# One core, a layer norm with a state-space convolution and eight experts: the convolution as three chains that take VectorE in turn, its bank handed out by readiness, its first steps in block two

## The chip, the cores and the metric

One core of one Trainium2 chip runs the whole program in one launch. The metric is the device time of one execution in microseconds (us). The kernel before took 2315.51, 2316.52 and 2318.74 us in three runs; the median is 2316.52 us.

## The reference

What is computed, cut to what matters (2048 tokens, width 512, 128 states, 8 experts of hidden width 1792, and K = 8, so that every token goes to every expert):

```
u: x = A_u                                # 2048 x 512
xn = layernorm(x)
# S4: a kernel of 2048 taps per channel, convolved causally with xn
dt = exp(log_dt); logdA = dt*(A_re + 1j*A_im); dB = dt*(B_re + 1j*B_im)
K[d, l] = sum_n (C[d,n] * exp(logdA[d,n]*l) * dB[d,n]).real
s4 = irfft(rfft(xn, 4096) * rfft(K, 4096))[:2048] + xn*Dskip
# experts
gates = softmax(xn @ w_gate)
moe = sum_e gates[:, e] * (silu(xn @ w1[e]) @ w2[e])
out = x + s4 + moe
```

## The kernel before, in words

**Products.** Every matmul operand is split into a high and a low half-precision part, and three products of the parts stand for one in single precision. The tokens are cut into 4 blocks `tb` of 512, the hidden width of an expert `e` into 7 pieces `pr` of 256, which are taken in 4 steps `d` (two pieces in a step, one in the last). `block(e, tb, d)` (L1969) forms the first layer's step with seven products instead of eight, from sums and differences of quarters of w1 and of the tokens; it writes three banks `hb0` to `hb2`, and ACT and VectorE make the halves `ahl` from them: ACT copies (L1996, L2011), the Silu into `fa`, `scB`, `scC` (L1504), the high half (L1508), and VectorE the low half (L1517). The second layer, `y` (L1471 to L1473, through `pop`), follows some slots later and reads `ahl`. In six "strong" blocks, (6,1), (6,2) and all four of expert 7, the second layer is made with seven products too: `block2` (L1827), `pop2` (L1726, output `z`), `evacuate2` (L1774). Their operands (`hs`, `f`, `ev`, `w2x`) lie in a second pool, p2, which `open_second` (L591) opens in the place of the pool p4 once S4 is done.

**The order is written by hand.** The program runs under a manual schedule: each engine's instructions stand in the order in which the Python code issues them. A block's step is four slots; `slot` (L1642) issues the matmuls of a product, some units of `y`, the high halves that are due, the low ones, pieces of weights that are being split (`work_on`, L641) and then S4 in the background: `bg_run` (L1396) takes the next steps of a generator as long as the estimated VectorE time of the slot, a fixed share of its estimated TensorE time, is not used up. A step yields its estimated VectorE cost, or `None` where it has to wait for another slot.

**Weights.** w1 comes raw in 512 KB pieces. Before, `piece_w1` (L538) formed the four sums of quarters in a tile `tw` (one 512-wide and two 256-wide VectorE operations, L504 to L506), split the three raw quarters (L493 on ACT, L496 on VectorE), and then split the sums. The pieces of experts 6's and 7's strong first blocks use `piece_w1x` (L568): the raw quarters are split first, the four sums are then made in their place (four 256-wide operations, L581), and split.

**S4** goes through 32 chunks `c` of 16 channels. VectorE makes a table of powers (`s4_tables`, L826: `ta`, `tt`, `table`), TensorE generates the taps from it (`kgen`, L871), ACT reads them, they go through DRAM (`s4_kernel_turn`, L892) and come back as `kt`; a power of two scales them (`s4_kscale` on VectorE, L902, from a total that TensorE sums up, `tot_k`, L183), ACT and VectorE split them (`kh`, L911 and L916). TensorE transforms them (`kf`, L954) and the tokens (`uf`, L940); VectorE multiplies in the short direction (`s4_conv`, L962 to L1007: `v3`, `k4`, `s3`, `z`), ACT and VectorE split `z` (`zh`, L1013, L1018), TensorE transforms back (`yp`, L1028), ACT copies it out (`ysb`, L1036), and SP's queue stores it (`ys`, L1037). All of `kgen`, `tot_k`, `kf`, `uf`, `yp`, the gates (`lg`) and the transposes share one small PSUM bank, tag "s4" of `ps_s`. Before, one generator `s4_pe` (L1094) asked for it in a fixed order, kf(c), yp(c-1), kgen(c+2), tot_k(c+2), uf(c+1), and `together` (L1057) ran VectorE's part of one c (table c+2, convolution c, tokens c+1) to its end before the next c. The first steps (basis, twiddles, dt, the DFT matrix) were part of the background too, `s4_all` (L1209).

At the end, `s4_final` (L1684) needs all `ys`; `gneg` (L2075) is the first VectorE operation on negated gates for the second half's evacuations.

## Time and profile before

| | |
|---|---|
| runs | 2315.51, 2316.52 (median), 2318.74 us |
| the profiled execution | 2316.77 us, span 2315.0 us (1.77 us lie outside of it) |
| mean granted TensorE clock | 0.998 |
| TensorE matmuls (PE) | busy 2297.5 us, 99% |
| weight loads (PEld) | 1644.3 us, 71% |
| VectorE (DVE) | 1885.4 us, 81% |
| ScalarE (ACT) | 1520.4 us, 66% |
| GpSimd (POOL) | 340.1 us, 15% |

How to read it: busy is the time in which an engine has an instruction in it. Matmuls are pipelined, so that the busy time of one is longer than the distance to the next; the distance of their starts is read from a timeline. A window's line gives the span, each engine's busy time in it with the number of instructions, the granted clock (1.00 is 2.4 GHz, 0.50 is 1.2 GHz), the DMA engines' share and the rate. A wait names the engine and line that waited, and what released it.

### The profile page before, as it was taken

Reading aid. Unit: us, or ns where it says so; the run is one execution under the profiler, and the core shown is the slowest. Engines: PE = TensorE matmul, PEld = TensorE weight load, DVE = VectorE, ACT = ScalarE, POOL = GpSimd, SP = SyncE. Lnnn points to the kernel's source line nnn. Section 1 sums busy time; section 2 is a strip of 40 time slices with the busy share of each in tenths; the row PEclk is TensorE's granted clock in tenths of the full one; section 3 lists DMA queues with packets and bytes.
Section 4 is the critical chain, followed back from the end, with each engine's and each line's share of the span. In section 5 each row is a group of like instructions: output and inputs, shape, how many; then the busy total and the mean of one; then the engine's idle time right before and its main releaser. Section 6 shows DMA issues by size and latency. Waiting matters only on the chain.

```text
span 2315.0 us, 51747 instructions
## 1 busy us (share of the span) xinstructions
PE 2297.5 (99%) x20809; PEld 1644.3 (71%) x20809; DVE 1885.4 (81%) x3984; ACT 1520.4 (66%) x2718; POOL 340.1 (15%) x397
## 2 busy tenths in 40 slices
PE   8999999999999999999999999999999999999999
PEld 4666666666666666666666666666666689779998
DVE  8864889989999899997999989998867664775445
ACT  7676666566665666666666666766667566775655
POOL 0001001121111211011110111111111111132111
PEclk9999999999999999999999999999999999999999
DMA  8597355774666746556465654576665563586353
GB/s 278 178 262 197 102 147 122 158 155 85 156 145 139 152 89 151 141 123 139 81 148 149 136 116 100 138 180 145 137 159 135 131 148 69 118 205 120 88 109 66
DMA packets 326817, 323.82 MB, mean 140 GB/s; under 512 B 183760, under 2 KB 221008, under 8 KB 326096
## 3 DMA queue, kind: packets, MB, share of 16 engines
q1 hardware_dynamic: 270272, 226.32, 33.3%
q0 software_dynamic: 56016, 93.94, 25.7%
q8 instruction: 162, 2.65, 0.5%
q14 instruction: 79, 0.65, 0.1%
q10 hardware_dynamic: 288, 0.26, 0.0%
HBM read 209.22 MB, written 66.58 MB: 119 GB/s over the span
## 4 chain that ended last, share of the span: by engine, by line
PE 95%; DVE 2%; ACT 2%; issue 1%; DMA 1%; POOL 0%; SPq 0%; DVEq 0%; ACTq 0%; POOLq 0%
PE hb L1488 34%; PE y L1471 13%; PE y L1473 13%; PE y L1472 13%; PE hb L1843 8%; PE z L1761 7%; PE hb L2047 2%; PE kgen L871 1%; PE yp L1028 1%; PE kf L954 1%; PE uf L940 1%; DMA scC<-sE 0%; PE tp L284 0%; DMA ut0c<-in_u_dram 0%; DVE hs L1876 0%
## 5 line engine op out<-in xcount | busy, mean ns | idle before, releaser
L1488 PE MATMUL hb<-xop,w1s 128*128 128x256 f16 x7350 | 865.6, 273 | 1.4 <-ACT scC L1996 1.0
L1488 PEld LDWEIGHTS <-w1s 128*128 128x128 f16 x7350 | 707.9, 98 | 133.6 <-issue 3.1
L1471 PE MATMUL y<-w2s,ahl 128*128 128x512 f16 x1456 | 552.1, 379 | 0.0
L1472 PE MATMUL y<-w2s,ahl 128*128 128x512 f16 x1456 | 552.1, 379 | 0.0
L1473 PE MATMUL y<-w2s,ahl 128*128 128x512 f16 x1456 | 552.1, 379 | 0.0
L1699 POOL DMA_DIRECT2D scC<-sE x124 | 111.6, 900 | 1346.7 <-ACT sE L1996 895.8
L1473 PEld LDWEIGHTS <-ahl 128*128 128x128 f16 x1456 | 142.2, 98 | 172.0
L1472 PEld LDWEIGHTS <-ahl 128*128 128x128 f16 x1456 | 142.3, 98 | 130.6
L1471 PEld LDWEIGHTS <-ahl 128*128 128x128 f16 x1456 | 142.3, 98 | 130.5
L1843 PE MATMUL hb<-xop,w1s 128*128 128x128 f16 x3528 | 212.7, 219 | 2.6 <-ACT scC L1853 1.6
L1504 ACT ACTIVATE fa<-hb,sc 128x512 f32<-128x512 f32 (+1 forms) x204 | 129.8, 636 | 126.2 <-PE hb L1488 125.8
L1843 PEld LDWEIGHTS <-w1s 128*128 128x128 f16 x3528 | 204.9, 98 | 8.0 <-issue 3.4
L1761 PEld LDWEIGHTS <-hs 128*128 128x128 f16 x1764 | 168.7, 98 | 20.0 <-DVE hs L1876 0.8
L1517 DVE SCALAR_TENSOR_TENSOR ahl<-fa,sc,ahl 128x512 f16<-128x512 f32 (+1 forms) x214 | 146.1, 683 | 30.8 <-ACT ahl L1508 30.6
L2011 ACT COPY hb<-hb 128x512 f32<-128x512 f32 x100 | 51.7, 517 | 173.7 <-PE hb L1488 173.5
L1699 POOL DMA_DIRECT2D scB<-sE x123 | 106.2, 863 | 401.5 <-ACT scB L1996 227.3
L1508 ACT ACTIVATE ahl<-fa,sc 128x512 f16<-128x512 f32 (+1 forms) x214 | 143.7, 672 | 7.7 <-DMA xnd<-xn 0.8
L859 DVE TENSOR_TENSOR table<-ta,tt 128x64 f32<-128x64 f32 (+2 forms) x192 | 132.0, 688 | 5.8
L853 DVE TENSOR_TENSOR ta<-table,zr 128x64 f32<-128x64 f32 (+2 forms) x192 | 131.8, 686 | 5.7
L995 DVE TENSOR_TENSOR s<-s,tm 128x672 f32<-128x672 f32 (+6 forms) x224 | 127.7, 570 | 7.7
L856 DVE TENSOR_TENSOR tt<-table,zi 128x64 f32<-128x64 f32 (+2 forms) x192 | 130.4, 679 | 0.0
L994 DVE TENSOR_TENSOR tm<-v,k 128x672 f32<-128x672 f32 (+6 forms) x224 | 126.6, 565 | 4.4
(332 smaller groups left out, 3299.6 us busy)
## 6 DMA issues: line engine op xcount, KB each, us to landing
xop<-xd SPq DMA_DIRECT2D x210, 256.0 KB, 3.7
pp<-in_w_dram SPq DMA_DIRECT2D x98, 512.0 KB, 4.4
raw<-in_w_dram SPq DMA_DIRECT2D x70, 512.0 KB, 4.3
oacc<-ye POOLq DMA_DIRECT2D x110, 256.0 KB, 6.3
scC<-sE POOLq DMA_DIRECT2D x87, 256.0 KB, 3.7
scB<-sE POOLq DMA_DIRECT2D x87, 256.0 KB, 3.6
raw<-in_w_dram SPq DMA_DIRECT2D x52, 256.0 KB, 3.6
raw<-in_w_dram SPq DMA_DIRECT2D x104, 128.0 KB, 4.0
```

What stands on the lines that cost most here:

```text
L853: V.tensor_tensor(ta, tin, zrv, op=ALU.mult)
L856: V.tensor_tensor(tt, tin[:, ::-1], ziv, op=ALU.mult)
L859: V.tensor_tensor(tout, ta, tt, op=ALU.add)
L1471: T.matmul(y, lhs[0], w2s[pr][:, 0, fh, :], start=(c == 0), stop=False)
L1472: T.matmul(y, lhs[0], w2s[pr][:, 1, fh, :], start=False, stop=False)
L1473: T.matmul(y, lhs[1], w2s[pr][:, 0, fh, :], start=False, stop=(c == NF - 1))
L1488: T.matmul(dst[:, q, :], w1s[pr][:, a, ORDER[e][wo], k * P:(k + 1) * P], xop[:, xo, b, k, :], start=(first_mm and q == 0 and n == 0), stop ...
L1508: S.activation(ahl[:, 0, :n], fa, AF.Copy, scale=scales[e][:, 3:4])
L1517: V.scalar_tensor_tensor(ahl[:, 1, :n], fa, sc[:, 3:4], ahl[:, 0, :n], op0=ALU.mult, op1=ALU.subtract)
L1699: nc.gpsimd.dma_start(dst, src, accum_op=ALU.add)
L1761: T.matmul(acc, t[:, a, q, :], w2_op(pr, p, b), start=(first and k == 0), stop=(c == NPR and k == 2), skip_group_check=True)
L1843: T.matmul(dst[:, q, :], w1s[pr][:, x, ORDER[e][wo], k * P:(k + 1) * P], xop[:, xo, b, k, tk], start=(first_mm and q == 0 and m == 0), sto ...
```

## The change

S4's matmuls come from four generators, each with its own conditions, which queue for the small bank; a copy out of the bank takes place at the earliest a slot after the matmuls. VectorE's part is three streams (tokens, tables, convolution), and `in_turn` takes a step of the first one that can go, in a sequence that depends on whether the tables are four chunks ahead. The total of a chunk's rows is column 256 of the next chunk's `kgen` bank, so `tot_k` is gone. The transformed taps get a tile of their own (`kr`), the convolution works on `k3`, and its result stands in `s3`; `kt` and `kh` have two buffers, the raw inputs `s4raw` one. One slot less lies between the scale and the high half of `kh`, and one less between the halves of `zh`. The basis, the twiddles and dt are issued in slots 30 to 44, which lie in block two. All w1 pieces take the form in which the sums replace the raw quarters, `tw` is gone, and every expert uses the order of products that the strong ones had. `fa` and `ev` move from their own buffers into others: `fa` into two of p4, and once p2 is open `fa` and `ev` into the twelve that `hs` rotates through. The six strong blocks are the same.

```diff
     def bank_free():
         if bank["out"]:
-            if clock["two"]:
+            if clock["two"] or bank["set"] == clock["slot"]:
                 return False
             take_bank()
         return clock["slot"] > bank["at"]
...
-    def w1_sums(e, pr, raw):
-
-        clock["dve"] += 1.4
-        tw = sb.tile([P, 4, 2 * P], F32, tag="tw", name=f"tw{e}_{pr}", bufs=1)
-        V.tensor_tensor(tw[:, 0:2, :], raw[:, 3:4, :].to_broadcast([P, 2, 2 * P]), raw[:, 0:3:2, :], op=ALU.subtract)
-        V.tensor_tensor(tw[:, 2, :], raw[:, 2, :], tw[:, 0, :], op=ALU.subtract)
-        V.tensor_tensor(tw[:, 3, :], raw[:, 1, :], tw[:, 2, :], op=ALU.subtract)
-        return tw
+    def w1_sums(raw):
+
+        clock["dve"] += 1.5
+        for o, x, y in ((0, 3, 0), (3, 3, 2), (2, 2, 0), (1, 1, 2)):
+            V.tensor_tensor(raw[:, o, :], raw[:, x, :], raw[:, y, :], op=ALU.subtract)
...
     def s4_kernel(c):
+        take_bank(lambda: s4_kernel_out(c))
+        kg = ps_s.tile([P, 512], F32, tag="s4", name=f"kgen{c}")
+        s4["kgen"] = kg
+        if c:
+            T.matmul(kg[:, 256:257], ones, s4["krow", c - 1].bitcast(BF16)[:, 1::2], start=True, stop=True)
+        if c == NCH:
+            return
...
     def s4_raw(g):
-        raw = p4.tile([P, 6, GD], F32, tag="s4raw", name=f"s4raw{g}", bufs=2)
+        raw = p4.tile([P, 6, GD], F32, tag="s4raw", name=f"s4raw{g}", bufs=1)
...
-    def together(gens):
...
+    def in_turn(x, tables, conv):
+
+        gens = {"x": x, "tables": tables, "conv": conv}
         while gens:
...
+            behind = s4.get("tabs", 0) - s4.get("zs", 0) < 4
+            for n in ("x", "tables", "conv") if behind else ("x", "conv", "tables"):
+                cost = next(gens[n], "end") if n in gens else None
+                if cost == "end":
+                    gens.pop(n)
+                elif cost is not None:
+                    yield cost
+                    break
+            else:
                 yield None
...
+    asked = []
+
     def bank_wait():
-        while not bank_free():
+        me = object()
+        asked.append(me)
+        while not bank_free() or asked[0] is not me:
             yield None
+        asked.pop(0)
...
+    def s4_pe_kf():
+        for c in range(NCH):
+            if c:
+                yield from until(("k3", c - 1))
+            yield from until(("kl", c))
+            yield from bank_wait()
+            s4_kf(c)
+            s4["kf", c] = now()
+            yield None
...
     def s4_ksplit(c):
...
-        if c:
-            yield from until(("kl", c - 1), more=0)
+        if c > 1:
+            yield from until(("kl", c - 2), more=0)
         s4_kernel_turn(c)
-        yield from bank_wait()
-        s4["kst", c] = pow2_total(s4["krow", c], 1, f"k{c}", lambda: s4.update({("read", c): now()}))
...
         yield from until(("read", c), more=0)
         s4_kscale(c)
         yield 0.6
-        yield None
-        if c:
-            yield from until(("kf", c - 1), more=0)
+        if c > 1:
+            yield from until(("kf", c - 2), more=0)
         s4_khigh(c)
...
         s4_zhigh(c)
         yield None
-        yield None
         s4_zlow(c)
...
-        polled.append(s4_pe())
-        for c in range(-2, NCH):
...
+        polled.extend((s4_pe_kf(), s4_pe_kernel(), s4_pe_back(), s4_pe_uf()))
+        yield from in_turn(s4_x_stream(), s4_table_stream(), s4_conv_stream())
...
-            fa = sb.tile([P, 2, TH], F32, tag="fa", name=f"fa{e}_{tb}_{d}_{fh}{th}")[:, :n]
+            late = "pool" in second_half
+            fa = (second_half["pool"] if late else p4).tile([P, 2, TH], F32, tag="hs" if late else "fa",
+                                                            name=f"fa{e}_{tb}_{d}_{fh}{th}", bufs=NHS if late else 2)[:, :n]
...
+    for n in range(30, 45):
+        at(n, lambda: next(first_part, None))
```

ACT, around the last chunk of S4. `ysb31` is the copy of the last chunk's result, `ahl5_3_3_00` and `fa5_3_3_00` belong to the last step of block (5,3), `sc6` and `w2s` to expert 6. Before:

```order
L1036 ACTIVATE ysb30_23885<-yp30_23580,ksc30_22633 128x256
L1036 ACTIVATE ysb31_23901<-yp31_23888,ksc31_23227 128x256
L1933 COPY hb1_103<-hb0_102 128x512
L1504 ACTIVATE scC6_0_3_23837<-scC6_0_3_23837,sc6_20970 128x256
L1508 ACTIVATE ahl6_0_3_11_23943<-scC6_0_3_23837,sc6_20970 128x256
L1940 COPY hb2_104<-hb1_103 128x512
L1865 ACTIVATE f11_6_1_0_24021<-hb0_102,sc6_20970 128x512
```

And of the change, on the same engine at the same tile `ysb31`:

```order
L1036 ACTIVATE ysb31_23103<-yp31_23039,kscale_139 128x256
L2003 COPY hb1_103<-hb0_102 128x256
L1504 ACTIVATE scC5_3_2_22998<-scC5_3_2_22998,sc5_17653 128x512
L1508 ACTIVATE ahl5_3_2_11_23115<-scC5_3_2_22998,sc5_17653 128x512
L498 ACTIVATE w2s1_96<-raw6_1_1_23031,sc6_20982 128x1024
L2013 COPY hb2_104<-hb1_103 128x256
L1504 ACTIVATE fa5_3_3_00_23152<-hb0_102,sc5_17653 128x256
L1508 ACTIVATE ahl5_3_3_00_23154<-fa5_3_3_00_23152,sc5_17653 128x256
```

The last result of S4 moved from the first strong block, (6,1), to the last step of block (5,3), a whole block earlier, and six instructions behind it stands the first tile of the second pool, `fa5_3_3_00`. Counted over the whole order of TensorE, the last `yp` stands at matmul 13,395 and stood at 13,959; the first `z` stands at 14,253 in both.

VectorE and ACT around the scale of chunk 3. `it_k3` and `ksc3` are the scale, `kh3` the taps of chunk 3 split, `table` and `ta5` the table of chunk 5, `ye` and `ahl` belong to the experts. Before, VectorE, and the ACT rows around the reader:

```order
L189 TENSOR_SCALAR it_k3_5922<-st_k3_5780 128x1
L190 TENSOR_SCALAR ksc3_5921<-it_k3_5922 128x1
L194 TENSOR_SCALAR ksc3_5921<-ksc3_5921 128x1
L1517 SCALAR_TENSOR_TENSOR ahl1_2_0_01_5868<-fa1_2_0_01_5866,sc1_2895,ahl1_2_0_01_5868 128x512
L834 COPY table_3319<-s4w2_5093 128x2x16
...
L1446 ACTIVATE ye1_4_6041<-y1_1_0_5166,gse1_3266 128x512
L1446 ACTIVATE ye1_5_6044<-y1_1_1_5170,gse1_3266 128x512
L911 ACTIVATE kh3_6048<-kt3_5594,ksc3_5921 128x256
L1996 COPY scC1_2_1_6070<-hb2_104 128x512
```

And of the change, the same rows of VectorE and of ACT:

```order
L845 TENSOR_TENSOR table_3068<-ta5_1_5531,tt5_1_5532 128x2x32x2
L192 TENSOR_SCALAR it_k3_5583<-st_k3_5504 128x1
L193 TENSOR_SCALAR kscale_139<-it_k3_5583 128x1
L197 TENSOR_SCALAR kscale_139<-kscale_139 128x1
L887 TENSOR_TENSOR ksb4_5506<-ksb4_5506,dskq_131 128x4
...
L1508 ACTIVATE ahl1_1_2_11_5613<-scC1_1_2_5472,sc1_3058 128x512
L181 COPY st_w2_0_5580<-tot_w2_0_5581 128x1
L909 ACTIVATE kh3_5624<-kt3_5255,kscale_139 128x256
L2013 COPY hb2_104<-hb1_103 128x256
L1504 ACTIVATE fa1_1_3_00_5648<-hb0_102,sc1_3058 128x256
```

The scale now stands one slot, not two, ahead of the ACT instruction that reads it, and the copy of bank `hb2`, on which TensorE's next product waits, stands right behind that instruction.

## Rows read from the trace of the kernel before

**Rows 1.** The first part of the page: busy time, share of the span and number of instructions of each engine.

```profile
PE 2297.5 (99%) x20809; PEld 1644.3 (71%) x20809; DVE 1885.4 (81%) x3984; ACT 1520.4 (66%) x2718; POOL 340.1 (15%) x397
```

**Rows 2.** Windows from 20 us to the end (us from the span's start: width, then busy time of each engine with its instructions, granted clock, DMA share, GB/s), cut where S4 begins to weigh on VectorE, at its last result and at the strong blocks.

```profile
20.00:260.00 240.00, 240.00 (x1695) 151.04 (x1693) 168.13 (x411) 170.64 (x279) 16.95 (x21) 1.00 0.70 207
260.00:520.00 260.00, 260.00 (x2207) 174.70 (x2206) 234.09 (x528) 167.00 (x312) 39.14 (x45) 1.00 0.61 142
...
780.00:1040.00 260.00, 259.97 (x2223) 175.59 (x2221) 247.66 (x511) 165.71 (x309) 37.44 (x43) 1.00 0.56 129
...
1300.00:1560.00 260.00, 259.72 (x2165) 175.29 (x2163) 245.51 (x537) 169.04 (x317) 35.61 (x41) 1.00 0.57 131
1560.00:1780.00 220.00, 220.00 (x1828) 149.10 (x1826) 173.14 (x364) 148.26 (x279) 31.30 (x36) 1.00 0.64 148
...
1838.00:1980.00 142.00, 140.44 (x1795) 127.03 (x1795) 86.10 (x158) 89.72 (x153) 22.70 (x26) 1.00 0.47 99
1980.00:2037.00 57.00, 55.92 (x426) 40.16 (x424) 42.62 (x67) 46.73 (x72) 10.38 (x12) 1.00 0.62 168
2037.00:2315.00 278.00, 273.17 (x3570) 250.87 (x3567) 152.30 (x269) 170.06 (x292) 55.13 (x63) 1.00 0.53 109
sum 2295.00, PE 2287.09 PEld 1635.58 DVE 1871.57 ACT 1509.13 POOL 339.40; mean PE 207.92 PEld 148.69 DVE 170.14 ACT 137.19 POOL 30.85
```

**Rows 3.** TensorE's waits over the whole span: the line that waited, what released it, us in total, times, longest.

```profile
PE tp L359 <- ACT xhl L349: 7.7, 1, 7.7
PE hb L1843 <- ACT scC L1853: 1.6, 2, 1.3
...
PE hb L1488 <- ACT scC L1996: 1.0, 2, 0.7
...
PE hb L1488 <- ACT hb L2011: 0.3, 1, 0.3
```

**Rows 4.** Timeline of TensorE in block (6,0) (start us, us, line, operation, operands, shape, count): the matmuls of a product between units of `y`.

```profile
1779.06 4.09 PE L1488 MATMUL hb<-xop,w1s 128*128 128x256 f16 x36
1782.99 0.38 PE L1471 MATMUL y<-w2s,ahl 128*128 128x512 f16 x1
...
1785.58 2.78 PE L1488 MATMUL hb<-xop,w1s 128*128 128x256 f16 x24
```

**Rows 5.** Lines of VectorE with the forms apart (count, busy us, mean ns of one, idle before): the sums of w1.

```profile
L504 DVE TENSOR_TENSOR tw<-raw 128x512 f32<-128x512 f32 x42 | 28.9, 688 | 0.7
L505 DVE TENSOR_TENSOR tw<-raw,tw 128x256 f32<-128x256 f32 x42 | 17.8, 425 | 1.4
L506 DVE TENSOR_TENSOR tw<-raw,tw 128x256 f32<-128x256 f32 x42 | 17.8, 425 | 1.4
L581 DVE TENSOR_TENSOR raw<-raw 128x256 f32<-128x256 f32 x28 | 11.8, 425 | 0.9
```

**Rows 6.** The tiles `kgen` and `yp` (count, duration ns min/median/max, first and last start us).

```profile
L871 PE MATMUL kgen<-table x2048: 218/219/244, 310.8 to 1733.9; 128*32 128x64 f32 x187
L1028 PE MATMUL yp<-zh,dfth x384: 218/219/220, 411.4 to 1832.5; 128*128 128x128 f16 x192
```

**Rows 7.** Timelines of TensorE (first two rows) and of ACT (the next two) in the first strong block, with the idle time before an instruction in brackets, and one wait of VectorE over the whole span.

```profile
1863.94 1.47 PE L1761 MATMUL z<-w2x,hs 128*128 128x256 f16 x12
1866.76 2.17 PE L1843 MATMUL hb<-xop,w1s 128*128 128x128 f16 x36 [1.34 <-ACT scC L1853]
...
1864.16 2.18 ACT L493 ACTIVATE w2x<-raw,sc 128x1024 f16<-128x1024 f32 x2
1866.24 0.47 ACT L1853 COPY scC<-hb 128x384 f32<-128x384 f32 x1
...
DVE gneg L2075 <- DMA ys<-ysb: 11.7, 1, 11.7
```

**Rows 8.** Lines of ACT with the forms apart (columns as in rows 5, behind the idle time what ended it).

```profile
L1504 ACT ACTIVATE fa<-hb,sc 128x256 f32<-128x256 f32 x50 | 23.7, 474 | 11.0 <-PE hb L1488 11.0
L2011 ACT COPY hb<-hb 128x256 f32<-128x256 f32 x25 | 9.0, 359 | 12.8 <-PE hb L1488 12.8
L1036 ACT ACTIVATE ysb<-yp,ksc 128x256 f32<-128x256 f32 x32 | 15.0, 467 | 15.5 <-PE yp L1028 10.3 <-DMA ys<-ysb 5.2
L1013 ACT ACTIVATE zh<-z 128x512 f16<-128x512 f32 x32 | 20.0, 625 | 2.4 <-DVE z L1007 2.4
```

**Rows 9.** Line 1037, the stores of S4's results: the issue on SP's queue (ns min/median/max, first and last start us), and the time from issue to landing.

```profile
L1037 SPq DMA_DIRECT2D ys<-ysb x32: 586/612/964, 419.7 to 1837.4; - x32
DMA to landing us min/median/max: 3.3/4.6/11.3
```

**Rows 10.** A line of TensorE (columns as in rows 5).

```profile
L871 PE MATMUL kgen<-table 128*32 128x64 f32 x2048 | 35.2, 221 | 0.1
```

**Rows 11.** A wait of SP's queue over the whole span, for the buffers of raw weights (columns as in rows 3).

```profile
SPq L480 <- ACT pp L489: 213.9, 43, 17.0
```

**Rows 12.** Windows of the first 20 us, columns as in rows 2.

```profile
6.80:10.20 3.40, 0.00 (x0) 0.00 (x0) 2.42 (x12) 1.17 (x3) 0.00 (x0) 0.63 1.00 341
10.20:13.60 3.40, 1.21 (x11) 0.95 (x12) 3.01 (x10) 2.27 (x4) 0.00 (x0) 0.50 0.96 293
13.60:17.00 3.40, 3.28 (x32) 2.77 (x29) 2.89 (x9) 3.33 (x6) 0.00 (x0) 0.50 0.95 304
17.00:20.40 3.40, 3.06 (x28) 2.21 (x27) 2.54 (x4) 3.40 (x7) 0.00 (x0) 0.87 1.02 375
```

More of the change, by code (lines that the diff above doesn't have):

```diff
@@ L112, in take_bank @@
             bank["at"] = clock["slot"]
-        bank["out"] = out
+        bank["out"], bank["set"] = out, clock["slot"]
     def bank_free():
         if bank["out"]:
-            if clock["two"]:
+            if clock["two"] or bank["set"] == clock["slot"]:
                 return False
@@ L144, in s4_moe_kernel @@
     dt_all = p4.tile([P, D], F32, bufs=1, name="dt_all")
-    dfth = p4.tile([P, 2, 8, P], F16, bufs=1, name="dfth")
+    dfth = p4.tile([P, 2, 2, 2, P], F16, bufs=1, name="dfth")
+    dftb = cp.tile([P, 2, 2, 2, P], F16, name="dftb")
+    kscale = cp.tile([P, NCH, 2], F32, name="kscale")
     def load_rest():
@@ L634, in can @@
             return False
-        if it.sums and len(it.steps) == it.n:
-            return not live["tw"]
-        if it.sums and len(it.steps) == 1:
-            return now() > it.at + (it.made[0] > 1)
+        if it.load is not None and it.n > 1 and len(it.steps) == 1 and it.made[1] == "w1":
+            return now() > it.at + (it.made[0] > 1 and "pool" not in second_half)
         return len(it.steps) == it.n or it.load is None or now() > it.at
     def work_on(limit):
+        if limit == 2 and bank["out"] and now() > bank["set"] + 2:
+            limit = 1
         clock["two"], n2 = False, limit
@@ L658, in work_on @@
                 break
-            if it.sums and len(it.steps) == it.n:
-                live["tw"], it.at = True, now()
             low = it.steps.pop(0)(it.raw)
@@ L667, in work_on @@
             if low:
-                lows.append((low, last, it.sums and last, it.made))
+                lows.append((low, last, it.made))
             elif last and it.load is not None:
@@ L678, in work_lows @@
         while lows:
-            low, last, sums, what = lows.pop(0)
+            low, last, what = lows.pop(0)
             low()
@@ L893, in s4_kernel_turn @@
         ksb = s4["ksb"]
-        kt = p4.tile([P, 4, 4 * NI], F32, tag="kt", name=f"kt{c}", bufs=1)
+        kt = p4.tile([P, 4, 4 * NI], F32, tag="kt", name=f"kt{c}", bufs=2)
         kd = kds[c % 2]
@@ L902, in s4_kscale @@
     def s4_kscale(c):
-        ks = s4["ks", c] = p4.tile([P, 2], F32, tag="ksc", name=f"ksc{c}", bufs=4)
+        ks = s4["ks", c] = kscale[:, c, :]
         pow2_scale(ks[:, 0:1], s4["kst", c], f"k{c}")
@@ new lines, in s4_pe_kernel @@
+    def s4_pe_kernel():
+        for c in range(NCH + 1):
+            if c < NCH:
+                yield from until(("tab", c))
+            if c:
+                yield from until(("ke", c - 1))
+            yield from bank_wait()
+            s4_kernel(c)
+            s4["kn", c] = now()
+            if c < NCH:
+                polled.append(s4_ksplit(c))
+            yield None
+    def s4_pe_kf():
+        for c in range(NCH):
+            if c:
+                yield from until(("k3", c - 1))
+            yield from until(("kl", c))
+            yield from bank_wait()
+            s4_kf(c)
+            s4["kf", c] = now()
+            yield None
@@ L1131, in s4_pe, with s4_pe_uf, s4_pe_back @@
+    def s4_pe_uf():
+        for c in range(NCH):
+            if c:
+                yield from until(("v3", c - 1))
+            yield from until(("ul", c))
+            yield from bank_wait()
+            s4_uf(c)
+            s4["uf", c] = now()
+            yield None
+    def s4_pe_back():
+        for c in range(NCH):
+            yield from until(("zl", c))
+            yield from bank_wait()
+            s4_back(c)
+            s4["back", c] = now()
+            yield None
         yield from bank_wait()
@@ L1138, in s4_ksplit @@
         yield 0.3
-        yield from hold(now())
-        if c:
-            yield from until(("kl", c - 1), more=0)
+        if c > 1:
+            yield from until(("kl", c - 2), more=0)
         s4_kernel_turn(c)
-        yield from bank_wait()
-        s4["kst", c] = pow2_total(s4["krow", c], 1, f"k{c}", lambda: s4.update({("read", c): now()}))
-        s4["total", c] = now()
         yield None
-        while ("read", c) not in s4:
-            bank_free()
-            if ("read", c) not in s4:
-                yield None
         yield from until(("read", c), more=0)
@@ L1437, in s4_moe_kernel @@
     units = []
-    ORDER = [(0, 1, 2, 3, 6, 5, 4) if (e, 0) in strong else tuple(range(7)) for e in range(E)]
+    ORDER = (0, 1, 2, 3, 6, 5, 4)
     ys = {}
@@ L1776, in evacuate2 @@
         g0, g1 = gates_e[e][:, i0:i0 + 1], second_half[e, "gneg"][:, i1:i1 + 1]
-        ev = second_half["pool"].tile([P, 2, TH], F32, tag="ev", name=f"ev{e}_{tb}_{a}", bufs=1)
+        ev = second_half["pool"].tile([P, 2, TH], F32, tag="hs", name=f"ev{e}_{tb}_{a}", bufs=NHS)
         t1, t7 = ev[:, 0, :], ev[:, 1, :]
@@ L1869, in high @@
         def high(p, f):
-            h = second_half["pool"].tile([P, 2, 4, P], F16, tag="hs", name=f"hs{p}_{e}_{tb}_{d}", bufs=12)
+            h = second_half["pool"].tile([P, 2, 4, P], F16, tag="hs", name=f"hs{p}_{e}_{tb}_{d}", bufs=NHS)
             S.activation(flat(h[:, 0]), flat(f), AF.Copy, scale=scales[e][:, 3:4])
```

268 lines of the change are left out of this document (111 added, 157 removed).

## The prediction

> **What bounds the kernel now.** I read the first part of the page for the engines, then windows for the stages, then TensorE's waits, then timelines where TensorE stood. The page gives TensorE 99% and VectorE 81% [rows 1]; the windows say it by stage. From 20 us to the end TensorE is busy 2287.09 of 2295.00 us [rows 2]: 7.91 us idle, of which 1.56 lie in 1838:1980, 1.08 in 1980:2037 and 4.83 in 2037:2315, behind S4's end. While VectorE carries S4, TensorE loses nothing in 260:520, 0.03 us in 780:1040, although VectorE is 95.3% busy there (247.66 of 260.00), 0.28 in 1300:1560. Its waits behind the start are single ones of at most 1.3 us [rows 3]. Nor is the busy time soft: in the timeline 36 matmuls of 256 columns go by in 3.93 us and the next 12 of 512 columns in 2.59 us [rows 4], 109 and 216 ns from start to start, twice the columns in twice the time. So TensorE bounds every stage after the first 20 us; the other engines count only where they make it wait.
>
> A rule of the Trainium skill speaks against the first reading: "Perfetto Trace Analysis", section "Identifying the Most-Contended Engine", says that the busy time of matmuls is no good measure of the room that is left, because they are pipelined, and wants the weight loads' share beside it; that share is 71% here. By the rule much could be gained; the start-to-start distances decide against it, and the sum stays the same.
>
> **The change part by part**, against the profiled execution's 2316.77 us (span 2315.0, 1.77 outside; 0.25 above the median of the runs).
>
> *Amount of work.* Counted over the two orders, TensorE issues the same number of matmuls with the same columns: 32 one-column `tot_k` become 32 one-column additions to a `kgen` bank. ACT's instructions are equal in number too; VectorE has 63 more. The w1 sums are most of that: 49 pieces were one 512-wide and two 256-wide operations, 0.688 + 0.425 + 0.425 = 1.54 us, and become four 256-wide ones as 28 instructions already are, 4 x 0.425 = 1.70 us [rows 5]. (42 are in the rows, 7 are the first expert's.) That is 49 x 0.16 = 8 us on VectorE over the span. It hides beside TensorE while VectorE keeps up; uncovered it would be 8 us, which belongs to the third rival. Here: 0.
>
> *S4 earlier and shorter.* By the order the last `yp` stands 564 matmuls earlier, 360 of 256 columns and 204 of 512: 360 x 0.109 + 204 x 0.216 = 83 us [rows 4]. The first `kgen` stands about 47 us earlier by the same count. S4 lies between 310.8 and 1832.5 [rows 6], 1521.7 us; it shrinks by 36 us, 2.4%. If this came out of every stretch alike, VectorE's densest one would go from 95.3% to 97.6%. There is room in 1560:1780, where it is busy 173.14 of 220.00, 78.7% [rows 2], and the budget per slot, a share of TensorE's time, is unchanged; so I take it from there, and TensorE gains nothing as it had no idle time there: 0. The starts before 260 us fall where VectorE is 70% busy (168.13 of 240.00).
>
> *A wait that goes (term a).* TensorE stood 1.34 us at 1866.76 for ACT's copy `scC`, which stood behind two splits of `w2x` taking 2.18 us [rows 7]. They are made when p2 is open, hence 83 us earlier, and by the order at least 43 us ahead of their use. VectorE's `gneg`, which waited 11.7 us for the last store [rows 7], goes with them. What is late next are the waits below 1.2 us [rows 3], which stay. a = -1.3 (0 to -1.6, the whole row of L1843 behind `scC`).
>
> *A wait that comes (term b).* p2 takes p4's place, so its first tile needs all that read p4 to be over, the last store `ys` among it. Before, 12 us passed on VectorE in this way without TensorE; now the first tile is `fa5_3_3_00` on ACT, a few instructions behind `ysb31`. Between them TensorE has 18 matmuls of 256 and 6 of 512 columns, 18 x 0.109 + 6 x 0.216 = 3.3 us, and the copy of the bank takes 0.36 [rows 8]: ACT arrives 3.7 us after the end of `yp`. The store is issued after the copy, 0.47 [rows 8] and 0.6 of queue, and lands after 4.6 in the median, 3.3 to 11.3 [rows 9]: 5.7. ACT is thus 2.0 us late. Behind it in its queue stand a high half, a split and, for TensorE, the copy that frees `hb0`, for which TensorE arrives with about 1.1 us to spare (units of `y` 1.3 and a product 0.65, less 0.36 and 0.47 on ACT). b = 2.0 - 1.1 = +0.9; 0 with a landing of 3.3, 7.6 with 11.3. I take the median's, as one store of 32 is drawn.
>
> The Trainium skill has a price for it: "DMA: Bandwidth & Descriptors", section "Anatomy of one DMA — SWDGE (gpsimd) path", fits 2.0 us plus the bytes over 436 GB/s, an estimate of 2.3 us for these 128 KB on another path than SP's queue; by it ACT would not be late, b would be 0 and the sum 2316.5. The trace's least of 32 is 3.3 us, so the measured landing stands.
>
> *The scale nearer to its reader (term c).* `kscale` on VectorE stands one slot ahead of ACT's `kh`. Durations added along both orders put at least 5.2 us between them before and at most 2.6 us in 9 of 32 chunks now. Where VectorE is behind by more, ACT waits, and behind ACT's `kh` stands the copy of `hb2`. The trace shows no wait of `kh` (its idle time is not among the rows of ACT's waits); the nearest row is `zh` behind `z`, ACT idle 2.4 us in all, in 2 of 32 [rows 8], where 7 stood this near: 0.34 us each. Nine times that is 3.1 if all of it reached TensorE; the copies `hb` cost TensorE 0.3 [rows 3]. I take c = +0.5 (0 to 3.1); below nothing is excluded, as no wait was there to lose. The halves of `zh`, nearer by one slot, have the same answer: ACT's half comes first and VectorE waits, not TensorE.
>
> *kgen nearer behind its table (term d).* By the same sums the least distance of a `kgen` behind VectorE's last table operation falls from 7.9 to 4.6 us, with 6.6 and 7.2 next. VectorE late by 7.9, which the trace does not show (`kgen` idle 0.1 [rows 10]), would cost 3.3 + 1.3 + 0.7 = 5.3. d = +0.5 (0 to 5.3), near to the row.
>
> *What I cost at nothing.* `s4raw` with one buffer makes SP wait for VectorE behind each load; SP already waits 213.9 us in 43 waits for buffers of other loads [rows 11], and weights stand further ahead in the new order; if that cover went, a split would be late, and TensorE with it, as in term a, by 1.3. `fa` from p4 has two buffers as before in number, from p2 twelve. The bank's copies stand a slot later at the earliest, and `bank_wait` has no instruction. The first 20 us hold the same waits, 7.7 us for `xhl` [rows 3] and the clock at 0.50 after it [rows 12]; iota, twiddles and dt in slots 30 to 44 lie after that: 0.
>
> Sum: 2316.8 - 1.3 + 0.9 + 0.5 + 0.5 = **2317.4 us**. Its own range, with landings up to 7 us and c and d to 2 each, is 2315 to 2321.
>
> **The rivals.**
> *The second pool opens late (slower).* One mechanism: the landing of the last store. For: ACT, on TensorE's path, now waits for what only VectorE waited for, and a landing of 11.3 us occurred. Against: the median is 4.6. It decides from a landing of 8.3 us on, where b is 4.6. With 11.3 the time is 2316.8 - 1.3 + 7.6 + 1.0 = 2324.1. After the wait of 7.7 us at the start the clock was 0.50 for two windows of 3.4 us [rows 12]; and 0.87 in the next; if it fell so here as well, 2 x 3.4 x 0.5 + 3.4 x 0.13 = 3.8 us more, 2328.
> *VectorE is over-fed (slower).* Three streams fill each slot's budget, where lockstep left holes, and VectorE gets 8 us more. For: 95.3% in the densest stretch, 97.6% if the shortening is even. Against: the budget is the same and rows 2 show no loss at 95.3%. By both orders the least distance from a low half `ahl` to its `y` is 7.9 us; once VectorE lags by more, TensorE goes at VectorE's pace. It decides where the work of the S4 stretch is over 100%; 1% over on 1485 us is 14.9 us: 2316.5 + 14.9 = 2331.
> *TensorE's idle time shrinks (faster).* For: 7.5 of the 7.9 us lie behind 1838 us [rows 2], where S4 is now long over, ACT and VectorE are freer and the weights are earlier. Against: only 1.3 of it can be tied to S4; the rest is in strong blocks that are the same, and the waits of TensorE after 20 us are by name ACT's copies within the block [rows 3]. It needs 4.6 of the 7.9 us; 5.5 us saved give 2311.
> *The change does not shorten S4* in time, though in the order: VectorE would have to lag by a slot in each chunk; that is the second rival at a smaller lag, and below 7.9 us of it gives 2317.
>
> **How the numbers follow.** Two executions of this kernel can differ by 0.2%, 4.6 us; that bounds "the same", 2311.9 to 2321.1. The forecast has 0.74, which includes the last rival at less lag; the late pool 0.09, VectorE over-fed 0.12, TensorE's idle time 0.05. Faster 0.05, same 0.74, slower 0.21. The range leaves out the faster case and most of VectorE's, 0.15 in all, and holds the bounds of a to d short of their joint ends: 2313.5 to 2325.
>
> **What would show it.** Right: in the profile after, the windows from 260 us to the end of S4 keep TensorE's idle time under 2 us with VectorE at 92 to 96%; the first `kgen` starts near 264 and the last `yp` near 1750; the wait of L1843 behind `scC` at `w2x` is gone; ACT idles some 2 us at the first `fa` from p2, released by `ys`, and TensorE 1 us after it. Wrong: a row of TensorE waiting on VectorE's `ahl` or `table` with more than 3 us in all (terms c and d, or the second rival); a wait of 5 us or more at the opening of p2, with a granted clock under 1.00 after it; or idle time in 2037:2315 other than 4.8 by more than 2 us, which would mean that what I took for unchanged in the strong blocks was not.

## The result, and the profile after

The changed kernel takes 2330.82 us (median of 4 runs, 2329.98 to 2331.57); before, on the same chips, 2317.36 (4 runs). The ratio is 1.0059, 95% interval [1.0043, 1.0075]: slower by 13.5 us, where 2317.4 us and "the same" had been forecast, and outside of the range, which ended at 2325.

The busy times of the page, which answer to [rows 1], show next to nothing:

```profile
PE 2299.8 (99%) x20809; PEld 1648.2 (71%) x20809; DVE 1901.1 (82%) x4047; ACT 1518.5 (65%) x2718; POOL 340.1 (15%) x397
```

The first line of the page's fourth part, the chain that ended last by engine, shows which engine to look at. Of the kernel before:

```profile
PE 95%; DVE 2%; ACT 2%; issue 1%; DMA 1%; POOL 0%; SPq 0%; DVEq 0%; ACTq 0%; POOLq 0%
```

and of the changed kernel:

```profile
PE 70%; DVE 21%; ACT 3%; DMA 3%; issue 2%; SPq 0%; DVEq 0%; ACTq 0%
```

The time that VectorE has in the chain went from 2% to 21%: its busy time hardly rose, but for long stretches the end now hangs on it. The windows say where TensorE lost (columns as in [rows 2]):

```profile
260.00:520.00 260.00, 257.23 (x2264) 174.33 (x2262) 238.07 (x537) 166.15 (x315) 39.18 (x45) 1.00 0.60 140
...
780.00:1040.00 260.00, 258.22 (x2166) 175.47 (x2165) 250.95 (x543) 165.76 (x306) 39.29 (x45) 1.00 0.59 131
1040.00:1300.00 260.00, 257.48 (x2192) 174.28 (x2191) 244.16 (x538) 167.46 (x311) 36.77 (x43) 0.99 0.54 122
1300.00:1560.00 260.00, 258.22 (x2214) 175.40 (x2212) 244.74 (x511) 170.13 (x321) 35.51 (x41) 1.00 0.60 136
1560.00:1780.00 220.00, 218.42 (x1709) 148.23 (x1708) 166.64 (x352) 146.96 (x274) 32.12 (x37) 1.00 0.63 147
```

The five windows of 260 us from 260 to 1560 together lose 11.6 us, where 0.4 were lost before. VectorE is 96.5% busy in the densest (250.95 of 260.00), and its work moved out of 1560:1780 (166.64 after 173.14). TensorE's waits, which answer to [rows 3], name VectorE nowhere between 260 and 1560 us (three short ones, 0.9 us in all, lie elsewhere, as before). Over the whole span:

```profile
PE hb L1486 <- ACT scC L1998: 9.0, 11, 2.1
PE tp L364 <- ACT xhl L354: 7.8, 1, 7.8
PE hb L1486 <- DMA xop<-xd: 2.4, 1, 2.4
...
PE hb L1486 <- ACT hb L2013: 1.3, 3, 0.5
```

A product waits for ACT to have copied a bank out (`scC`, `hb`). What holds ACT is told by the chain of one stretch, 1176 to 1190 us (start us, us, what; the pieces of that stretch in order of time):

```profile
1180.36 0.42 DVE s L1006
1180.78 0.35 DVE s L1007
...
1181.15 0.63 ACT zh L1013
1181.78 0.27 ACT hb L2013
1182.05 0.41 ACT fa L1504
...
1184.36 0.23 ACT zi L788
...
1185.32 0.92 ACT w1s L498
1186.24 0.40 ACT kh L909
```

VectorE is late with `z`; ACT, which takes its instructions in order, stands at `zh` for it; behind `zh` stand the copy of `hb2`, the Silu, the sines of the basis (`zi`), a split of w1 and `kh`, and only behind these the copy `scC` on which TensorE's next product waits. ACT's own rows (the idle time before an instruction in brackets):

```profile
1181.15 0.63 ACT L1013 ACTIVATE zh<-s 128x512 f16<-128x512 f32 x1 [0.75 <-DVE s L1007]
1186.54 0.35 ACT L1998 COPY scC<-hb 128x256 f32<-128x256 f32 x1
```

TensorE in the same stretch (a timeline's rows):

```profile
1182.11 1.47 PE L1486 MATMUL hb<-xop,w1s 128*128 128x256 f16 x12 [0.44 <-ACT hb L2013]
1186.94 2.68 PE L1486 MATMUL hb<-xop,w1s 128*128 128x256 f16 x12 [2.07 <-ACT scC L1998]
```

The second row shows a second loss: 12 matmuls took 2.68 us in the place of 1.47. Behind the two waits the granted clock fell to the lower level:

```profile
1180.00:1186.90 6.90, 4.42 (x28) 2.53 (x26) 6.73 (x18) 6.02 (x14) 0.00 (x0) 1.00 0.30 95
1186.90:1190.30 3.40, 3.36 (x15) 2.10 (x15) 3.30 (x7) 1.88 (x5) 0.86 (x1) 0.52 0.95 302
1190.30:1193.70 3.40, 3.40 (x32) 2.53 (x31) 3.23 (x10) 2.37 (x4) 0.86 (x1) 0.98 0.74 159
```

3.4 us at 0.52 cost 1.6 us.

VectorE's lateness is only a part of these 2.51 us. ACT idles 0.75 us for it and has no idle time from 1181.15 to the copy at 1186.54, so with `z` ready the copy would have come at most 0.75 us earlier; the rest is ACT's own work, which this order gathers in front of the copy. Four places in 260:1560 have this form (660 to 665, 815, 1182 to 1187 and 1491 us). TensorE lost 6.7 us there; ACT's idle time for VectorE right ahead of them, 1.56, 1.66, 0.75 and 1.21 us, can answer for at most 4.2 of it.

The waits of ACT for VectorE between 260 and 1780 us add up to 14.6 us in 13 places, and to 4.7 in 6 before:

```profile
ACT zi L788 <- DVE bf L785: 5.4, 4, 1.8
ACT w1s L498 <- DVE raw L509: 4.5, 4, 1.4
ACT zh L1013 <- DVE s L1007: 3.3, 3, 1.6
ACT kr L956 <- DVE s L989: 1.2, 1, 1.2
ACT kh L909 <- DVE kscale L193: 0.2, 1, 0.2
```

The single wait for `xop` is another matter. SP's queue at that place (start us, us, and what was issued):

```profile
283.94 0.43 SPq L894 DMA_DIRECT2D kd<-ksb  x1
289.80 1.76 SPq L896 DMA_DIRECT2D kt<-kd  x4
...
293.72 1.94 SPq L1994 DMA_DIRECT2D xop<-xd  x1
...
296.49 3.49 SPq L1994 DMA_DIRECT2D xop<-xd  x6
```

and TensorE:

```profile
298.17 1.05 PE L1486 MATMUL hb<-xop,w1s 128*128 128x256 f16 x8 [2.43 <-DMA xop<-xd]
```

With the first steps in block two the first chunk's taps go through DRAM just when the tokens of the next block are due: the load `kt` waits in SP's queue until `kd` has landed, and the load of `xop` stands behind it:

```profile
SPq L896 <- DMA kd<-ksb: 5.3, 1, 5.3
```

The sum is this: the span grew by 13.8 us. TensorE's idle time from 20 us on rose from 7.9 to 19.2 us (2308.8 less 2289.6 busy), by 11.3: 11.2 more in 260:1560, 2.0 more in 1560:1840, 1.9 less behind it. 1.6 us are the lower clock, and 0.9 are spread.

### The profile page after: what moved, and what is told of

Read it like the earlier page. It is cut to its first block, busy times and chain, and to the rows that moved or that the text cites. A ratio compares the mean times of both kernels' runs of the same rounds, so it can differ in the third digit from the quotient of the medians.

```text
span 2328.8 us, 51814 instructions
## 1 busy us (share of the span) xinstructions
PE 2299.8 (99%) x20809; PEld 1648.2 (71%) x20809; DVE 1901.1 (82%) x4047; ACT 1518.5 (65%) x2718; POOL 340.1 (15%) x397
## 4 chain that ended last, share of the span: by engine, by line
PE 70%; DVE 21%; ACT 3%; DMA 3%; issue 2%; SPq 0%; DVEq 0%; ACTq 0%
PE hb L1486 23%; PE y L1470 9%; PE y L1469 9%; PE y L1471 9%; PE hb L1845 8%; PE z L1763 8%; DVE ahl L1517 3%; DVE tm L994 2%; DVE s L995 2%; DVE ta L841 2%; DVE tt L844 2%; PE hb L2049 2%; DVE w1s L501 2%; DVE table L845 1%; DVE raw L509 1%
## 5 line engine op out<-in xcount | busy, mean ns | idle before, releaser
L2013 ACT COPY hb<-hb 128x512 f32<-128x512 f32 x100 | 51.8, 518 | 177.2 <-PE hb L1486 177.0
L2003 ACT COPY hb<-hb 128x512 f32<-128x512 f32 x100 | 51.9, 519 | 125.2 <-PE hb L1486 124.6
```

## The experiments

Two theories at first. Theory 1: VectorE is over-fed by the three streams and falls behind; ACT waits for it and TensorE for ACT. Theory 2: the new form of the w1 pieces holds the raw buffers longer, so that ACT and SP wait. A third, the luck of where instructions meet, came with the second run. The runs came in three groups, e1 to e4, e5 to e8 and e9 to e12, with medians of before of 2316.42, 2316.13 and 2315.87 us. The changed kernel was not measured again beside them; its 2330.82 us stand against 2317.36. So what a run gained is given as the difference of the two distances, each to its own before (13.5 us for the change).

**Less work for VectorE per slot (e1).**

```diff
-    SHARE = 0.96
+    SHARE = 0.92
```

> The changed kernel with one number changed: the share of TensorE's estimated time that VectorE may be given per slot is 0.92 in the place of 0.96. Theory 1 (VectorE is over-fed: the three streams fill each slot to the budget, VectorE lags behind TensorE, ACT's instructions that read fresh VectorE results stand in front of the copies that free the banks): with 4% less per slot the lag goes, the idle time of TensorE between 260 and 1560 us falls from 11.6 us to under 3 us, and the time is 2317 to 2321 us; the last yp moves from 1763 to some 1800 to 1825 us. Theory 2 (the new form of the w1 pieces holds the raw buffers longer, so that SP's queue and ACT wait for them): the budget is not its cause, the waits at xop and at raw stay, and the time is 2327 to 2331 us.

Measured: 2318.47 us, 1.001 [1.0001, 1.0019] of before. That is 2.1 us over its own before: of the 13.5 us 11.4 are gone, by one number. The chain has VectorE at 3%, and ACT waits for VectorE 1.8 us in the place of 14.6. Windows of this run, from 260 to 1560 and on to 1840 us:

```profile
260.00:1560.00 1300.00, 1296.81 (x10956) 879.29 (x10953) 1189.96 (x2594) 840.73 (x1562) 193.45 (x223) 1.00 0.59 134
1560.00:1840.00 280.00, 279.90 (x2288) 190.62 (x2287) 234.43 (x470) 188.12 (x345) 41.66 (x48) 1.00 0.63 144
```

VectorE went from 1228.55 to 1189.96 us in the first window, and from 206.68 to 234.43 in the second. The last `yp` now starts at 1833.8 us, where it was before the change (1832.5), though the first `kgen` still starts early, at 265.5; 1800 to 1825 us had been expected. Idle time in 260:1560 is 3.19 us, just over the 3 expected. A wait for `xop` of 1.6 us stays, and the wait at `w2x` of 1.3 us ahead of the first strong block is back. Theory 2 asked for 2327 to 2331 us and falls as the main cause.

**One slot more ahead of zh (e2).**

```diff
             yield from until(("back", c - 1), more=0)
+        yield None
         s4_zhigh(c)
```

> The changed kernel with one slot more between the last VectorE operation of a chunk's z and ACT's high half of it (zh). Theory 1 in a narrow form (one reader is to blame: zh stands in ACT's queue while VectorE is still at z): the waits at 659.9 and 664.45 us (0.54 and 1.78 us) and at 1182 and 1187 us (0.44 and 2.07 us, and 1.6 us by the lower clock behind the second) go, 6.4 us together, and the time is 2324 to 2325 us. Theory 2 (w1 form): nothing of its waits is touched, 2329 to 2332 us. Theory 3 (where things collide is luck of positions): other places take over, the time is anything from 2323 to 2335 us, and the waits by line are of the same kinds as before.

Measured: 2322.18 us, 1.0025 [1.0014, 1.0035]. No wait of ACT at `zh` is left, and of the waits at 660 and 1187 us one of 0.29 is left. The time is 5.8 us over its before, 7.7 us gained where 6.4 had been laid to `zh`: under theory 1's 2324, within theory 3's range. The wait at `xop` is 3.5 us here. The edit did more than move one reader: the last `yp` starts at 1800.7 us in the place of 1762.6, so VectorE was fed more slowly as well.

**zh and the sines of the basis a slot later (e3).** The edit above, and

```diff
-        act_later.append((clock["slot"] + 1, sines))
+        act_later.append((clock["slot"] + 2, sines))
```

> The changed kernel with both readers of fresh VectorE results one slot later on ACT: zh, and the sines of the basis (zi), which waited for VectorE 5.4 us in four places. Theory 1 in the narrow form: 1.3 us at 814.69 go as well, so 2322 to 2324 us, and no wait of ACT on VectorE at zh or zi is left. Theory 1 in the wide form (the lag itself matters, and the next reader waits in their place): 2326 to 2331 us, with ACT waiting at w1s, kr or kh in their place. Theory 2 (w1 form): 2328 to 2331 us.

Measured: 2322.58 us, 1.0031 [1.0019, 1.0043]. ACT waits for VectorE only 2.3 us now (12.9 with `zh` alone), yet the time is the same; the granted clock was below 1.00 behind the wait at `xop`. Here too S4 became slower: VectorE is busy 1194.24 us in 260:1560 (1228.55 in the change), nearly as little as with the share at 0.92, and the last `yp` starts at 1832.8 us. Inconclusive as to `zi`.

**The w1 form in the kernel before (e4).** All its w1 pieces as `piece_w1x`, `piece_sums` in place, the order of products that belongs to it:

```diff
-        a = [piece_w1(e, pr, made("p", d)) for d, prs in enumerate(DQS) for pr in prs]
+        a = [piece_w1x(e, pr, made("p", d)) for d, prs in enumerate(DQS) for pr in prs]
```

> The kernel before with the w1 pieces alone changed: all of them split the raw quarters first, make the four sums in their place and split these, with the order of products that belongs to it; S4 and all else as before. Theory 2 (w1 form): most of the loss is here, 4 to 13 us over before, 2321 to 2330 us, with TensorE waiting for xop behind SP's loads of raw weights, and ACT at the split of the sums. Theory 1 (over-fed VectorE): 8 us more of VectorE's time, most of it hidden as the S4 stream gives way; 2316 to 2320 us.

Measured: 2318.27 us, 1.0009 [1.0, 1.0019]: 1.9 us, and no wait at `xop`. The form costs little by itself, as theory 1 had it.

**The share at 0.94 (e5).**

```diff
-    SHARE = 0.96
+    SHARE = 0.94
```

> The changed kernel with the share at 0.94, between 0.92 (2318.5 us) and 0.96 (2330.8 us). If the time hangs on VectorE's lag, which grows without bound only near full, the loss is convex in the share: 2319 to 2322 us, VectorE 94 to 95% busy in its densest window, S4's last yp near 1800 us, and the first strong block's wait at w2x (1.34 us) gone. If the loss goes linearly with the share, 2324 to 2326 us. If 0.92 was a lucky alignment, anything up to 2331 us.

Measured: 2321.18 us, 1.0021 [1.0012, 1.0031], 5.1 us over its before, within the 2319 to 2322 us of the convex reading. Of it 3.4 us are the start of S4 (0.34 at 269.8, 3.11 for `xop` at 299.3), and behind the second wait the granted clock was low, which cost some 1.5 us more:

```profile
300.00:303.40 3.40, 3.40 (x15) 1.56 (x13) 3.30 (x9) 2.31 (x4) 0.00 (x0) 0.57 1.00 293
```

The wait at `w2x` is 0.30 in the place of 1.34. The last `yp` starts at 1829.8 us, not near 1800.

**The kernel before, over-fed (e6).**

```diff
-    SHARE = 0.96
+    SHARE = 1.02
```

> The kernel before with the share at 1.02 in the place of 0.96, its lockstep and all else as it was. If the budget binds in it too, over-feeding alone makes it slow: VectorE above 96% in its densest windows, the same waits of ACT at zh and zi, and 2325 to 2345 us. If the lockstep leaves holes that the budget doesn't fill (a chunk's matmuls stand in one fixed order and the streams wait for each other), VectorE gets hardly busier and the time stays at 2316 to 2320 us: then it is the three streams that filled the holes.

Measured: 2343.11 us, 1.012 [1.0103, 1.0137]. The old lockstep becomes slow too, by 27 us, without one line of the change, as the first branch had it. Its longest waits of ACT for VectorE, 260 to 1780 us:

```profile
ACT w1s L493 <- DVE tw L506: 12.6, 3, 7.1
ACT zh L1013 <- DVE z L1007: 10.5, 5, 4.5
ACT zi L800 <- DVE bf L797: 9.6, 4, 3.0
```

But it is not only that way: TensorE also waits for VectorE itself, at `yp`, and for a copy ahead of `tot_k`, which the change no longer has:

```profile
PE hb L1488 <- ACT scC L1996: 5.8, 6, 1.7
PE tot_k L183 <- ACT ysb L1036: 5.4, 1, 5.4
PE yp L1028 <- DVE zh L1018: 5.2, 2, 3.4
```

Its window:

```profile
260.00:1560.00 1300.00, 1280.33 (x10876) 865.28 (x10877) 1206.42 (x2604) 829.45 (x1536) 190.80 (x219) 1.00 0.58 129
```

VectorE is busy 92.8% there (1206.42 of 1300), no more than in the kernel before (1210.69), and 95.8% in its densest window (249.12 of 260.00), where over 96% had been expected: how full it is on the mean does not tell the two apart. How far behind it runs does (the table below), though not in every run.

**The first steps back in the background (e7).**

```diff
-    for n in range(30, 45):
-        at(n, lambda: next(first_part, None))
```

> The changed kernel without the first steps in block two: they are made by the background as before, so that S4's first kgen lies near 310 us again, share 0.96. If the wait of 2.43 us at 298 us (the product waits for xop, whose load stands in SP's queue behind the wait of the first kt for its kd) comes from the early start, it goes, and with it the 0.34 us at 269 us: 2327 to 2329 us, with the rest of the loss as it was. If it comes from the w1 form's longer hold on raw buffers, it stays and the time is 2330 to 2332 us.

Measured: 2324.3 us, 1.0034 [1.0021, 1.0047]. The waits at 269 and 298 us are gone, as the first reading said; the 5.3 us gained are more than their 2.8, and the time is under the 2327 to 2329 us expected. The first `kgen` starts at 315.8 us and the last `yp` at 1822.8: of the 70 us by which the change ended S4 earlier, 60 go with the early first steps. Beside e4, whose w1 form and first steps are the same, this run shows what the streams and the rest do to VectorE at the same share (e4 first, then e7):

```profile
260.00:1560.00 1300.00, 1298.60 (x10981) 878.45 (x10979) 1206.69 (x2630) 845.22 (x1564) 194.03 (x223) 1.00 0.59 134
260.00:1560.00 1300.00, 1293.05 (x10995) 876.59 (x10994) 1224.16 (x2657) 840.38 (x1565) 192.74 (x222) 1.00 0.59 133
```

VectorE has 17.5 us more work there, and TensorE 5.6 us more idle time.

**The slots behind the scale and zh put back (e8).**

```diff
         yield 0.6
+        yield None
         if c > 1:
...
         s4_zhigh(c)
         yield None
+        yield None
         s4_zlow(c)
```

> The changed kernel with the two slots put back that it took away, between the scale and kh and between the halves of zh. The prediction's term c said that the nearer scale costs 0.5 us (0 to 3.1): 2327.5 to 2330.5 us. The trace shows one wait of ACT for the scale, 0.2 us, so theory 1 expects no gain there: 2329 to 2332 us, with the waits at zh and zi as they were.

Measured: 2324.61 us, 1.0037 [1.0024, 1.0051]. 5.0 us gained, though ACT's wait for the scale was 0.2 us and still is: all theories were wrong here. Four quite different edits (e2, e3, e7, e8) have now given 5 to 8 us each, which looks like the luck of one order. It is not shown by them, as all four also slow S4 down: the last `yp` starts 38 to 70 us later than in the change (1800.7, 1832.8, 1822.8 and 1803.0 us).

**The taps of the first chunk behind the tokens (e9).** The share 0.94, and

```diff
         s4_skip(c)
         yield 0.3
+        if c == 0:
+            yield from hold(now() + 4)
```

> The changed kernel with the share at 0.94 and the trip of the first chunk's taps through DRAM (kd, kt) four slots later, so that the load of kt, which waits in SP's queue for kd to land, stands behind the loads of xop in place of in front of them. Theory (the early start costs through SP's queue): the wait for xop at 299 us, 3.1 us in the run with 0.94 alone, is gone; 2321.2 - 3.1 = 2318 us, give or take 1.5 by where else ACT and VectorE collide. If the load of xop is late for another reason (raw weights), the wait stays and the time is 2321 us.

Measured: 2317.14 us, 1.0005 [0.9996, 1.0015], 1.3 us over its before, 3.8 us less than with the share alone, and within the 2318 give or take 1.5 expected. No wait at `xop` is left, and the clock behind that place is 1.00. The load of `xop` comes first and 3 us earlier:

```profile
290.20 2.61 SPq L1996 DMA_DIRECT2D xop<-xd  x1
...
293.40 3.13 SPq L1996 DMA_DIRECT2D xop<-xd  x6
...
305.76 1.75 SPq L896 DMA_DIRECT2D kt<-kd  x4
```

and in the window

```profile
260.00:1560.00 1300.00, 1297.96 (x11052) 881.74 (x11050) 1212.30 (x2635) 842.91 (x1565) 193.41 (x222) 1.00 0.60 134
```

With VectorE as full as before the change (1212.30, 1210.69 then) TensorE loses 2.0 us there. The last `yp` starts at 1826.1 us, 6 us earlier than before, but the first `kgen` starts 45 us earlier (265.7): at this share S4 takes longer than in the lockstep (1560 us, 1522 then), so the 6 us come from the start and not from the streams.

**The same, with zh a slot later (e10).**

> The same with zh one slot later too: it takes the waits of ACT on VectorE that are left and might beat both kernels: 2314 to 2317 us if the waits at scC go (1.6 and 0.8 us in the run with 0.94), as the first strong block has its w2x early; 2317 to 2320 us if others come in their place.

Measured: 2318.84 us, 1.0013 [1.0003, 1.0023]: a wait of 1.35 us at `w2x` is back; why is not shown, as S4 ends at 1830.5 us here and at 1829.8 in e5, where that wait is 0.30. Neither version beats the kernel before.

**The share half a per cent to either side (e11, e12).** `SHARE = 0.955` and `SHARE = 0.965`.

> The changed kernel with the share at 0.955, half a per cent below its own, to tell the steady cost of a full VectorE from the luck of where instructions fall. If the time is a smooth function of the share: 2327 to 2330 us. If a part of the 13.5 us is the luck of this one order: 2322 to 2326 us, as the runs with one slot moved gave, with the granted clock at 1.00 all along.

> The changed kernel with the share at 0.965, half a per cent above its own. Smooth: 2332 to 2335 us. Luck of the order: anything between 2323 and 2335 us, and not tied to the run at 0.955.

Measured: 2327.66 us, 1.0048 [1.0033, 1.0063], and 2326.94 us, 1.0044 [1.0029, 1.0059]. They are 11.8 and 11.1 us over their before. The smooth reading holds at 0.955 and fails at 0.965, where it asked for 2332 to 2335 us; S4 ends there as in the change (last `yp` at 1765.7 us), so this is the run that speaks for the luck of the order. That 0.965 is faster than 0.96 is not clear of noise: the intervals of the two ratios overlap. Both have a wait of 3.0 us at `xop`.

How far VectorE runs behind can be taken from each trace: for each of its instructions, its start less the start of the matmul that stands last ahead of it in the program's order. Counted are those over 6 us, where that matmul starts between 260 and 1560 us:

| run | share | us | over 6 us behind | ACT waits for VectorE, 260:1780 | TensorE idle, 260:1560 | last yp at |
|---|---|---|---|---|---|---|
| e1 | 0.92 | 2318.5 | 0 | 1.8 | 3.19 | 1833.8 |
| e5 | 0.94 | 2321.2 | 0 | 3.2 | 5.14 | 1829.8 |
| e9 (kt later) | 0.94 | 2317.1 | 0 | 4.0 | 2.04 | 1826.1 |
| e10 (and zh) | 0.94 | 2318.8 | 4 | 6.3 | 1.59 | 1830.5 |
| e11 | 0.955 | 2327.7 | 14 | 9.3 | 6.41 | 1798.1 |
| the change | 0.96 | 2330.8 | 70 | 14.6 | 11.61 | 1762.6 |
| e2 (zh) | 0.96 | 2322.2 | 67 | 12.9 | 6.35 | 1800.7 |
| e3 (zh, zi) | 0.96 | 2322.6 | 72 | 2.3 | 5.90 | 1832.8 |
| e7 (first steps) | 0.96 | 2324.3 | 56 | 7.1 | 6.95 | 1822.8 |
| e8 (slots back) | 0.96 | 2324.6 | 14 | 9.6 | 6.17 | 1803.0 |
| e12 | 0.965 | 2326.9 | 135 | 16.1 | 6.91 | 1765.7 |
| before | 0.96 | 2316.5 | 39 | 4.7 | 0.42 | 1832.5 |
| before, e4 (w1 form) | 0.96 | 2318.3 | 0 | 3.8 | 1.40 | 1834.8 |
| before, e6 | 1.02 | 2343.1 | 420 | 39.0 | 19.67 | 1824.7 |

No column orders the times. At a share of 0.94 or less VectorE hardly runs behind and the time is 1.3 to 5.1 us over before; over-fed by far (e6) the lag and the time are both the largest; but e2 and e3 run behind as often as the change and lose half as much. Nor is 6 us the lag that matters: at 12 of the 13 places where ACT waited for VectorE in the change, VectorE was 2.0 to 5.8 us behind. What a lag costs hangs on which reader on ACT meets it, and on what ACT has in front of its next copy.

## Why the prediction was wrong

*The step that failed* is the one on S4 earlier and shorter: "There is room in 1560:1780 [...] and the budget per slot, a share of TensorE's time, is unchanged; so I take it from there, and TensorE gains nothing as it had no idle time there: 0." An unchanged budget was taken for an unchanged load. At the same share the lockstep put less into the full stretches than the three streams do: 1206.69 us of VectorE in 260:1560 in e4, 1224.16 in e7, 1228.55 in the change. VectorE's work did go out of 1560:1780, but into the full stretches, and the price was not 0: 11.2 us of idle time there, of which 2.8 belong to the start of S4 (below), and 1.6 us of clock.

*The rival* that VectorE is over-fed had 0.12 and its 2331 us is nearly the measured time, but by another way. It let the lag reach TensorE through `ahl` and `y`, from 7.9 us on. No `y` waited so. The lag reached TensorE through ACT, which takes in order what VectorE's results release, with the copies of the banks behind; there lags of 4.6 to 5.8 us were enough at three of the four places (8.8 at the fourth). That the time agrees is chance: the 1% in it was a unit, not a measurement.

*Term a* came true: the wait of 1.34 us behind `scC` at `w2x` is gone, and the other one of that row, 0.23 us, is 0.22 now. Not foreseen: the wait of 1.05 us for `hb` (L1940) in the strong blocks is gone as well, and one of 0.20 (L1935) came elsewhere in them.

*Term b*, 0.9 us at the opening of the second pool, measured 1.58: ACT waited for `ys` only 0.39 us, and the rest came from the three splits of weights that stand around the same copies, in the trace's rows at 1770 to 1777 us.

*Terms c and d*, 0.5 each. ACT waited 0.2 us for the scale, and no `kgen` waited for its table. In the sum they were held for the kind of wait that did the damage, a reader on ACT near behind VectorE, but at the wrong readers: `zi` 5.4 us, the sums of w1 4.5 and `zh` 3.3 were late, `kh` was not. `zh` was priced as the nearest row and then left aside, and the w1 sums were costed by VectorE's time alone, not as a wait of ACT for sums that VectorE makes behind its own split.

*Cost at nothing.* The sentence "The first 20 us hold the same waits [...]; iota, twiddles and dt in slots 30 to 44 lie after that: 0" looked at those steps, and not at what they let start earlier: the first trip of the taps through DRAM, past which SP's load of `xop` had to go. 2.43 us here, 3.11 with the share at 0.94, shown by e7 (gone with the early steps) and e9 (gone with the order in SP's queue). The DMAs that an earlier step sets off were not followed through the queue that they go past. The 8 us of w1 sums, put at 0 too, cost 1.9 us alone in e4 (by its interval 0 to 4.4).

*What would show it.* The first `kgen` at 264 (263.9) and the last `yp` near 1750 (1762.6, the lost time included) were right; the bound of 2 us idle up to the end of S4 was the row that failed.

The first reading itself held: TensorE bounds the kernel, and no kernel here was faster than the one before. The Trainium skill, "Perfetto Trace Analysis", section "Identifying the Most-Contended Engine", holds occupancy for a fair measure of how close VectorE is to its roofline. It does not tell what a full VectorE costs: here 93.3% in 260:1560 (1212.30 of 1300) go with 2317.1 us in e9, and 92.8% with 2343.1 us in e6, which is another kernel.

What stays open is how much of the 13.5 us is the luck of this one order. Seven orders of the changed kernel with shares from 0.955 to 0.965 (the change itself, e2, e3, e7, e8, e11, e12) gave 2322.2 to 2330.8 us, the change itself the most. That every one of them is 5.8 us or more over before, and none at 0.94 or less over 5.1, is shown; the part of each cause in the 13.5 us is not. One ledger stands on record: 1.9 us over before with the w1 form (e4), 8.2 with all but the early first steps (e7), 13.5 with all. It is no separation, as each step moves the order too, and e7 differs from e4 in the bank's hand-out, slots and buffers besides the streams. Nor was ACT's order alone changed so that less work stands in front of its copies; that would test the 2.5 us (6.7 less 4.2) which VectorE's lateness does not answer for.

## What to carry to other kernels

Where a hand-written order fills a second engine up to a budget, ask what left the budget unfilled so far; a change that closes the holes is a change of load, and the first experiment is the budget's own number. An engine that runs behind can reach the bounding one not by its own results, but through the engine that reads them in order with other work behind; so list the readers that stand nearest behind it, and what stands between them and the next copy that the bounding engine needs. Look at the chain's share by engine beside busy time: it names the engine, not the size of the loss (VectorE's 19% in e7 went with 2324.3 us, its 12% in e6 with 2343.1). And follow a step that is moved earlier to the first DMA that it lets go, and to what stands behind that in its queue.

## What the runs showed that was not expected

The time is rough in the order: an edit that puts back two slots, at one of which ACT had waited 0.2 us (e8), gained 5.0 us, and half a per cent more share (e12) cost nothing. Two waits of TensorE, 0.44 and 2.07 us within 5 us, had 3.4 us at a granted clock of 0.52 behind them, while the wait of 2.43 us at 298 us and the one of 1.78 us at 664 us, 4.6 us behind one of 0.54, left it at 1.00. At the place of the wait for `xop` the length does not decide in other runs either: 3.49 us in e2 left the clock at 1.00, while behind 2.21 us in e8 and 2.99 us in e11 it was 0.61 and 0.63 in 300:303.4. In e3 a wait of 2.66 us there had 12 matmuls behind it that took 2.74 us in the place of 1.47.
